# Other layouts of q, k and v on the partitions, at the start of a fused attention and MoE kernel

## The chip, the cores and the metric

The kernel runs on one core of a Trainium2 chip. The metric is the device time of one execution in microseconds. Before the change three runs took 1101.92, 1102.78 and 1104.07 us (median 1102.78 us).

## The reference

Three stages follow each other: linear attention with an RMS norm, a "max of three" MLP (below MoE 1), and a dense mixture of four experts (MoE 2). All data are float32.

```python
# q, k, v: (4, 8, 576, 64); g_norm: (64,)
kv  = einsum('bhsd,bhse->bhde', k, v)
out = einsum('bhsd,bhde->bhse', q, kv)
x   = out / sqrt(mean(out*out, -1) + 1e-6) * g_norm      # -> (2304 tokens, 512)
h   = maximum(maximum(x @ w1, x @ w2), x @ w3)           # MoE 1, d_ff = 768
x   = h @ w_out
p   = probs / (probs.sum(-1) + 1e-9)                     # 4 experts, d_ff = 1024
out = sum_e p[:, e] * (maximum(x @ e_w1[e], 0) @ e_w2[e])
```

## The kernel before

Products of the two MoE stages are taken with operands split in a high and a low part (`fp32r`), some by a seven-product scheme. They fill the time from about 60 us to the end and the change doesn't touch them. It touches the attention, which fills the first 60 us, and the order of the tokens inside a tile of 128.

**Groups and tiles.** Each of the four batches has 576 tokens. The first 512 make two groups of 256 tokens, each two tiles of 128; the last 64 tokens of two batches share one tile. `groups` numbers them 0 to 9: 0, 1 (batch 0), 2 (the rests), 3, 4 (batch 1), 5, 6 (batch 2), 7 (the rests again), 8, 9 (batch 3). The rests of all four batches are loaded and transposed together, as group 2. A group of 256 tokens is laid out with two neighbouring tokens on each of 128 partitions.

**Loads.** `load_q` (line 132) fetches a group with one DMA of 512 KB, whose contiguous pieces are two tokens of a head, 512 bytes; the rests come with four DMAs of 128 KB (line 138), each to 32 partitions. `load_kv` (line 169) fetches four heads of one batch of k and of v, here called a chunk: four neighbouring tokens on each of 128 partitions (pieces of 1 KB, line 175) and, by a second DMA of 64 KB, the last 64 tokens on 64 partitions (pieces of 256 bytes, line 176). So a chunk is four DMAs and 1.18 MB. The first chunk is cut finer (`load_first`). All these come from SyncE's queue (SP), except two from ScalarE's queue in the first chunk.

**Order of loads.** The list `order` (line 926) gives it: `w` is a weight of MoE 1, `k01` chunk 1 of batch 0, `q1` group 1. After each step of the work `pump` issues on from it, as far as buffers are free: six for q groups, three chunks.

**Order of work.** The list `steps` (line 972) is the program order of every engine. Its letters: `Kbc` is one pair of heads of k^T v for batch b (`att_kv`, line 272; five accumulating matmuls for each head), `Tn` the transposes of q group n (`att_T`, line 295), `On` the product with kv and the sums of squares (`att_O`), `Nn` the norm (`att_N`), `Xn` the transposes of the result (`att_X`), `S` the split of x, `c`, `d`, `s` the conversion of a weight, `A`, `H`, `P` parts of MoE 1. The beginning is `K00 K01 c0 d0 K02 K03 T1 O1 T0 N1 K10 K11 O0 X1 N0 T2 T3 K12 K13 X0 O3 S0 N3 O2 K20 T4 O4 s0 N2 T5 N4 K21`. In `T2` the rests are first copied by POOL into head-contiguous order (line 303), then transposed from the copy.

**Norm.** `att_O` sums squares into `ss` and computes `a = ss/64 + 1e-6` on VectorE; `att_N` takes the square root on ScalarE from `ss` with a scale and a bias, so beside `a`, and VectorE goes on with both.

Of the kernel before, what the change touches and what calls it, by code (L numbers as in the profile page):

```python
# [8 lines left out]
F32 = mybir.dt.float32  # L9
# [3 lines left out]
AF = mybir.ActivationFunctionType  # L13
# [8 lines left out]
def tile_attn_moe_moe2(  # L22
# [23 lines left out]
    nc = tc.nc  # L46
    B, H, S, D = q.shape
    NT, DM = out.shape
    FF = w1.shape[1]
    E, _, EF = e_w1.shape  # L50
    P = 128
# [5 lines left out]
    TPB = T // P  # L57
    NTILE = NT // P
    NPAIR = H // 2
    KC = S // P  # L60
    EPS = 1e-6
    WARM = 16

    def f32(ap):
# [25 lines left out]
    eps = cst.tile([P, 1], F32, name="eps")  # L90
    p_all = cst.tile([P, NTILE, E], F32, name="p_all")
# [24 lines left out]

    tiles = []
    groups = []
    SB = S // 256 * 256
    for b0 in range(0, B, 2):  # L120
        for b, s0 in ((b0, 0), (b0, 256), (b0, None), (b0 + 1, 0), (b0 + 1, 256)):
            groups.append((b, s0, len(tiles)))
            if s0 is None:
                tiles.append([out[bb * S + SB : (bb + 1) * S, :] for bb in (b, b + 1)])
            else:
                rows = out[b * S + s0 : b * S + s0 + 256, :].rearrange("(p r) d -> r p d", r=2)
                tiles += [[rows[0]], [rows[1]]]

    q_sb = {}
    kv_sb = {}  # L130

    def load_q(pool, gi):
        b, s0, _ = groups[gi]
        t = pool.tile([P, H, 2, D], F32, tag="q", name=f"q{gi}", bufs=6)
        if s0 is None:
            n = P // B
            for bb in range(B):
                nc.sync.dma_start(
                    out=t[bb * n : (bb + 1) * n], in_=q[bb, :, SB:S, :].rearrange("h (p r) d -> p h r d", r=2)
                )  # L140
        else:
            nc.sync.dma_start(
                out=t, in_=q[b, :, s0 : s0 + 256, :].rearrange("h (p r) d -> p h r d", r=2)
            )
        q_sb[gi] = t

    HALF = P // 2
    KS = P * KC  # L150

    def load_first(pool):

        ends = []
        for src, nm, eng in ((k, "k", nc.sync), (v, "v", nc.scalar)):
            t = pool.tile([P, 4, KC + 1, D], F32, tag="kv", name=f"{nm}0_0", bufs=6)
            rows = src[0, 0:4]
            parts = [
                (t[:, 2 * i : 2 * i + 2, 0:KC, :], rows[2 * i : 2 * i + 2, 0:KS, :].rearrange("h (p c) d -> p h c d", c=KC))
                for i in range(2)  # L160
            ]
            eng.dma_start(out=parts[0][0], in_=parts[0][1])
            eng.dma_start(out=t[0:HALF, :, KC, :], in_=rows[:, KS:S, :].rearrange("h p d -> p h d"))
            ends.append(parts[1])
            kv_sb[nm, 0, 0] = t
        for o, i in ends:
            nc.sync.dma_start(out=o, in_=i)

    def load_kv(pool, b, c):
        if (b, c) == (0, 0):  # L170
            return load_first(pool)
        for src, nm in ((k, "k"), (v, "v")):
            t = pool.tile([P, 4, KC + 1, D], F32, tag="kv", name=f"{nm}{b}_{c}", bufs=6)
            rows = src[b, 4 * c : 4 * c + 4]
            nc.sync.dma_start(out=t[:, :, 0:KC, :], in_=rows[:, 0:KS, :].rearrange("h (p c) d -> p h c d", c=KC))
            nc.sync.dma_start(out=t[0:HALF, :, KC, :], in_=rows[:, KS:S, :].rearrange("h p d -> p h d"))
            kv_sb[nm, b, c] = t

# [91 lines left out]
    def att_kv(kvb, b, c, eng=""):  # L272
        if c == 0:
            kv_ps[b] = banks[7]
        ps = kv_ps[b]
        kt, vt = kv_sb["k", b, c // 2], kv_sb["v", b, c // 2]
        for i in range(KC + 1):
            for h in range(2):
                o = ps[h * D : (h + 1) * D, c * D : (c + 1) * D]
                n = P if i < KC else HALF  # L280
                hh = c % 2 * 2 + h
                nc.tensor.matmul(o, kt[0:n, hh, i, :], vt[0:n, hh, i, :], start=(i == 0), stop=(i == KC))
        if c == NPAIR - 1:
            dst = kvb[b % 2][:, 0 : H * P].rearrange("p (c h n) -> p c h n", h=2, n=P)
            for h in range(2):
                src = ps[h * D : (h + 1) * D, 0 : NPAIR * D].rearrange("p (c e) -> p c e", e=D)
                e = eng[2 * h :] or "aa"
                copy(e[0], dst[0:D, :, h, 0:D], src)
                copy(e[1], dst[D:P, :, h, D:P], src)

    qT = {}
    TAIL = 2
    xtok = {}

    def att_T(pool, gi, eng="aa"):


        pair = groups[gi][1] is None
        t = pool.tile([P, 4, P, 2] if pair else [P, 2, 4, P], F32, tag="qp" if pair else "qT", name=f"qT{gi}", bufs=1 if pair else 2)
        qs = q_sb.pop(gi)  # L300
        if pair:
            qr = pool.tile([P, 2, H, D], F32, tag="qr", name="qr", bufs=1)
            nc.gpsimd.tensor_copy(out=qr, in_=qs.rearrange("p h r d -> p r h d"))
        for i in range(2):
            ps = bank("a").rearrange("p (c n) -> p c n", n=P)
            for c in range(4):
                src = qr[:, i, 2 * c : 2 * c + 2, :] if pair else qs[:, 4 * i + c, :, :]
                nc.tensor.transpose(ps[:, c, :], src, ident)
            copy(eng[i], t[:, :, :, i] if pair else t[:, i], ps)
        qT[gi] = t  # L310

    def att_O(pool, kvb, gi):
        b, s0, _ = groups[gi]
        qt = qT[TAIL] if s0 is None else qT.pop(gi)
        ps = [bank("acc") for i in range(1 if s0 is None else 2)]
        xt = pool.tile([P, 2, H, D], F32, tag="xt", name=f"xt{gi}", bufs=3)
        if s0 is None:
            nbank = 1
            for c in range(NPAIR):
                for bb in range(2):  # L320
                    rows = slice(bb * HALF, (bb + 1) * HALF)
                    toks = slice((b + bb) * P // B, (b + bb + 1) * P // B)
                    pair = kvb[(b + bb) % 2][:, 2 * c * P : 2 * c * P + 384]
                    nc.tensor.matmul(
                        ps[0][rows, c * P : (c + 1) * P], qt[:, c, toks, :],
                        pair.rearrange("p (h n) -> p h n", h=2)[:, :, 0:D], start=True, stop=True,
                    )
            dst = [xt[:, 0]]
        else:
            nbank = 2  # L330
            for h in range(H):
                nc.tensor.matmul(
                    ps[h // 4][:, h % 4 * P : (h % 4 + 1) * P], qt[:, h // 4, h % 4, :],
                    kvb[b % 2][:, h * P : (h + 1) * P], start=True, stop=True,
                )
            dst = [xt[:, :, 4 * i : 4 * i + 4, :].rearrange("p r h d -> p h r d") for i in range(2)]
        o = [ps[i].rearrange("p (n d) -> p n d", d=D) for i in range(nbank)]

        def small(nm):
            return smp.tile([P, nbank, 8], F32, tag=nm, name=f"{nm}{gi}")  # L340

        ss, a = small("ss"), small("a")
        for i in range(nbank):
            sq = xt[:, i]
            nc.scalar.activation(out=sq, in_=o[i], func=AF.Square)
            nc.vector.reduce_sum(out=ss[:, i, :], in_=sq, axis=AX.X)
        nc.vector.tensor_scalar(out=a, in0=ss, scalar1=1.0 / D, scalar2=EPS, op0=ALU.mult, op1=ALU.add)
        xtok[gi] = (xt, ss, a, o, dst, small)

    def att_N(gi):  # L350
# [1 line left out]
        nbank = len(o)  # L352
        s0, rr = small("s0"), small("rr")

        nc.scalar.activation(out=s0, in_=ss, func=AF.Sqrt, scale=1.0 / D, bias=eps)
        nc.vector.reciprocal(out=rr, in_=s0)
        nc.vector.tensor_tensor(out=rr, in0=a, in1=rr, op=ALU.mult)
        nc.vector.tensor_tensor(out=rr, in0=rr, in1=s0, op=ALU.add)
# [529 lines left out]
    def load_probs():  # L888
        for gi, (b, s0, t) in enumerate(groups):
            if s0 is None:  # L890
                for r in range(2):
                    nc.sync.dma_start(
                        out=p_all[r * HALF : (r + 1) * HALF, t, :], in_=probs[(b + r) * S + SB : (b + r + 1) * S, :]
                    )
            else:
                r0 = b * S + s0
                nc.sync.dma_start(
                    out=p_all[:, t : t + 2, :], in_=probs[r0 : r0 + 256, :].rearrange("(p r) e -> p r e", r=2)
                )

    def norm_probs():
# [6 lines left out]
    with tc.manual_schedule():  # L908
# [13 lines left out]
        for t in kvb:  # L922
# [1 line left out]


        order = (
            "w k00 k01 q1 q0 k10 q3 q2 k11 q4 q5 k20 w q6 k21 w k30 k31 q8 w q9"
        ).split()
        free = {"q": 6, "k": 3}

        def pump():
            late = []
# [51 lines left out]
        for st in steps:  # L984
# [10 lines left out]
                    conv2(worder[n], *en)  # L995
            elif kind == "T":
                att_T(xq, *at, *en)
                free["q"] += 1
            elif kind == "K":
                att_kv(kvb, *at, *en)  # L1000
                free["k"] += at[1] % 2
# [274 lines left out]
```

## Time and profile before

| what | value |
| --- | --- |
| median of 3 runs | 1102.78 us |
| the profiled execution, its own time | 1102.58 us |
| its span (first to last instruction) | 1100.8 us |
| TensorE (PE) busy | 1070.6 us, 97% |
| VectorE (DVE) busy | 768.7 us, 70% |
| ScalarE (ACT) busy | 593.9 us, 54% |
| GpSimd (POOL) busy | 238.8 us, 22% |
| granted TensorE clock, mean | 0.993 of full speed |

Busy shares are means over the whole span. The attention at the start has limits of its own, so tables by stretches of time are read for it. A matmul of float32 shows as two records in the trace. "L282" is line 282 of the kernel before.

### The profile page before, as it was taken

To read this page: it belongs to the slowest core of one execution; us is meant where nothing else is said; L and a number is where in the kernel's file an instruction comes from. 1 tells how busy PE (TensorE), PEld (TensorE's weight loads), DVE (VectorE), ACT (ScalarE), POOL (GpSimd) and SP (SyncE) were. 2 spreads that over 40 slices of the span, in tenths; PEclk is the share of its full clock that TensorE was granted. 3 is DMA by queue.
4 is the path that set the end of the run, shared out by engine and by line. 5 is a ranking of instruction groups with operands and counts; after the bars stand their busy time and mean duration, and the time that the engine had idled before them with its cause. 6 is when DMAs were issued, how large, how long until landed. Compare 5 with 4: busy or idle time off the path is not lost.

```text
span 1100.8 us, 19219 instructions
## 1 busy us (share of the span) xinstructions
PE 1070.6 (97%) x7318; PEld 1051.7 (96%) x7318; DVE 768.7 (70%) x1434; ACT 593.9 (54%) x1257; POOL 238.8 (22%) x269
## 2 busy tenths in 40 slices
PE   7889999999999989999999999999999999999997
PEld 6779999999999879999999999999999999999997
DVE  3889985667656879776676666667667666666556
ACT  3544224335343666665665566666566566556652
POOL 1336633330101101111202212212212220221121
PEclk8999999999999999999999999999999999999999
DMA  9945555431610877388569579759949957956875
GB/s 259 295 148 162 181 182 178 132 119 53 210 58 20 328 270 266 142 311 240 90 221 272 119 169 285 182 100 290 250 77 277 277 86 227 271 116 166 235 222 115
DMA packets 109820, 209.17 MB, mean 190 GB/s; under 512 B 13856, under 2 KB 67104, under 8 KB 109728
## 3 DMA queue, kind: packets, MB, share of 16 engines
q1 hardware_dynamic: 89248, 169.34, 46.4%
q0 software_dynamic: 19472, 37.76, 19.2%
q8 instruction: 57, 0.93, 0.3%
q10 hardware_dynamic: 1008, 0.85, 0.3%
q14 instruction: 35, 0.29, 0.1%
HBM read 137.93 MB, written 69.99 MB: 189 GB/s over the span
## 4 chain that ended last, share of the span: by engine, by line
PE 63%; DVE 0%; issue 0%; DVEq 0%
PE bank L878 32%; PE bank L617 30%; DVE wr L579 0%; DVE xr L500 0%; DVE fa L861 0%; DVE hr L653 0%; DVE hr L651 0%; DVEq L1271 0%
## 5 line engine op out<-in xcount | busy, mean ns | idle before, releaser
L878 PE MATMUL bank<-wr 128*128 128x256 f32 x1701 | 263.5, 283 | 0.4 <-DVE wr L579 0.4
L878 PEld LDWEIGHTS bank<-wr 128*128 128x128 f32 x1701 | 239.9, 190 | 0.6 <-DVE wr L579 0.6
L617 PE MATMUL bank<-rb,wl 128*128 128x384 f32 x1032 | 211.6, 340 | 4.2 <-DVE rb L500 2.3
L671 ACT ACTIVATE fa<-bank 128x384 f32<-128x384 f32 x192 | 94.7, 493 | 171.4 <-PE bank L617 169.5
L617 PEld LDWEIGHTS bank<-rb,wl 128*128 128x128 f32 x1032 | 176.0, 189 | 7.4 <-DVE rb L500 3.5
L617 PE MATMUL bank<-xr,wl 128*128 128x384 f32 x864 | 175.8, 337 | 1.7 <-DVE xr L500 1.1
L617 PEld LDWEIGHTS bank<-xr,wl 128*128 128x128 f32 x864 | 144.9, 188 | 3.6 <-DVE xr L500 2.5
L653 DVE TENSOR_TENSOR wr<-fa,wr 128x384 fp32r<-128x384 f32 x131 | 72.3, 552 | 50.8 <-ACT wr L646 50.7
L878 PE MATMUL bank<-wr,hr 128*128 128x256 f32 x558 | 91.0, 281 | 0.0
L836 POOL DMA_DIRECT2D out_dram<-w2s x48 | 48.1, 1027 | 193.0 <-DVE ob L861 145.0
L836 POOL DMA_DIRECT2D out_dram<-ob x48 | 47.7, 1033 | 166.8 <-DVE w2s L861 90.6
L878 PEld LDWEIGHTS bank<-wr,hr 128*128 128x128 f32 x558 | 80.5, 188 | 0.0
L646 ACT ACTIVATE wr<-fa 128x384 fp32r<-128x384 f32 x152 | 78.2, 529 | 2.0 <-DVE fa L661 0.5
L878 PE MATMUL bank<-wr,xr 128*128 128x256 f32 x405 | 67.9, 281 | 0.0
L760 DVE TENSOR_TENSOR fa<-bank,fa 128x384 f32<-128x384 f32 x54 | 29.9, 554 | 51.8 <-ACT fa L757 36.5
L836 POOL DMA_DIRECT2D out_dram<-fa x37 | 34.2, 1054 | 123.9 <-DVE fa L861 68.9
L694 DVE TENSOR_TENSOR fa<-bank,fa 128x384 f32<-128x384 f32 x48 | 26.7, 557 | 49.2 <-PE bank L617 49.2
L683 DVE TENSOR_TENSOR fa<-bank,fa 128x384 f32<-128x384 f32 x48 | 26.7, 557 | 48.0 <-ACT fa L671 47.2
L859 ACT ACTIVATE ob<-bank,p_all 128x256 f32<-128x256 f32 x102 | 48.3, 474 | 21.7 <-PE bank L878 20.0
L859 ACT ACTIVATE w2s<-bank,p_all 128x256 f32<-128x256 f32 x104 | 49.3, 474 | 18.8 <-PE bank L878 18.7
L617 PE MATMUL bank<-op,wl 128*128 128x384 f32 x288 | 58.7, 339 | 0.6 <-ACT fa L671 0.6
L878 PEld LDWEIGHTS bank<-wr,xr 128*128 128x128 f32 x405 | 59.0, 188 | 0.0
(207 smaller groups left out, 2041.9 us busy)
## 6 DMA issues: line engine op xcount, KB each, us to landing
rb<-op_d SPq DMA_DIRECT2D x42, 768.0 KB, 5.1
xr<-op_d SPq DMA_DIRECT2D x42, 768.0 KB, 7.0
out_dram<-w2s POOLq DMA_DIRECT2D x47, 256.0 KB, 5.9
out_dram<-ob POOLq DMA_DIRECT2D x46, 256.0 KB, 5.2
op<-op_d SPq DMA_DIRECT2D x14, 768.0 KB, 7.9
stage_a<-in_moe_w_dram SPq DMA_DIRECT2D x18, 512.0 KB, 4.0
w1s<-in_moe_w_dram SPq DMA_DIRECT2D x30, 256.0 KB, 3.6
out_dram<-fa POOLq DMA_DIRECT2D x30, 256.0 KB, 5.9
```

The lines of the kernel that those rows point to most:

```text
L617: nc.tensor.matmul(out, w[wi][:, c * P : (c + 1) * P], y[yi][:, c, :], start=(i == 0 and k in begin), stop=(i == 5), skip_group_check=k no ...
L646: nc.scalar.activation(out=ops[key][0], in_=src, func=AF.Relu if relu else AF.Copy)
L653: nc.vector.tensor_tensor(out=lo, in0=src, in1=f32(hi), op=ALU.subtract)
L671: nc.scalar.activation(out=out, in_=in_, func=func)
L683: nc.vector.tensor_tensor(out=t22, in0=x, in1=t22, op=ALU.add)
L694: nc.vector.tensor_tensor(out=t12, in0=x, in1=t12, op=ALU.add)
L760: nc.vector.tensor_tensor(out=mx[done] if i == 0 else t, in0=x, in1=t, op=ALU.add)
L836: nc.gpsimd.dma_start(out=rows, in_=src, accum_op=ALU.add)
L859: nc.scalar.activation(out=o, in_=piece(ps, i), func=AF.Copy, scale=pe)
L878: nc.tensor.matmul(piece(ps, i), h[hi][:, i * P : (i + 1) * P], w[wi], start=fresh, stop=last, skip_group_check=True,)
```

## The change

q of a batch is loaded as four tokens on each of 128 partitions, 512 tokens in two DMAs of four heads each (pieces of 1 KB); tiles and output rows follow that order. The rests come by eight DMAs of 64 KB, one for each batch and token of a pair (pieces of 256 bytes), already in the order that the transposes want, and POOL's copy is gone. k and v come with six tokens on each of 96 partitions, one DMA for each chunk and operand (pieces of 1.5 KB), without the second DMA; the matmuls contract over 96 rows, six for each head in place of five. The list of loads and the count of free q buffers follow; a q buffer comes free when both its groups are transposed. `a` now lies in the place of `ss`, and the square root reads it.

```diff
-    KC = S // P
+    KC = 6
+    KP = S // KC
-    SB = S // 256 * 256
+    SB = S // 512 * 512
+    by_r = [out[b * S : b * S + SB, :].rearrange("(p r) d -> r p d", r=4) for b in range(B)]
...
-                rows = out[b * S + s0 : b * S + s0 + 256, :].rearrange("(p r) d -> r p d", r=2)
-                tiles += [[rows[0]], [rows[1]]]
+                r0 = s0 // P
+                tiles += [[by_r[b][r0]], [by_r[b][r0 + 1]]]
...
+    def load_q(pool, b):
+        if b == B:
+            t = pool.tile([P, 2, H, D], F32, tag="qe", name="q_ends", bufs=1)
             n = P // B
             for bb in range(B):
+                for r in range(2):
+                    nc.sync.dma_start(
+                        out=t[bb * n : (bb + 1) * n, r],
+                        in_=q[bb, :, SB:S, :].rearrange("h (p r) d -> r p h d", r=2)[r],
+                    )
+            q_sb[TAIL] = t
+            return
+        t = pool.tile([P, H, 4, D], F32, tag="q", name=f"q{b}", bufs=3)
+        for i in range(2):
+            hs = slice(i * H // 2, (i + 1) * H // 2)
+            nc.sync.dma_start(out=t[:, hs], in_=q[b, hs, 0:SB, :].rearrange("h (p r) d -> p h r d", r=4))
+        for n, gi in enumerate(gi for gi, g in enumerate(groups) if g[0] == b and g[1] is not None):
+            q_sb[gi] = t[:, :, 2 * n : 2 * n + 2, :]
+
+    def load_kv(pool, b, c):
+        first = (b, c) == (0, 0)
         ends = []
+        for src, nm in ((k, "k"), (v, "v")):
+            t = pool.tile([P, 4, KC, D], F32, tag="kv", name=f"{nm}{b}_{c}", bufs=6)
+            rows = src[b, 4 * c : 4 * c + 4].rearrange("h (p c) d -> p h c d", c=KC)
+            if first:
+                (nc.sync if nm == "k" else nc.scalar).dma_start(out=t[0:KP, 0:2], in_=rows[:, 0:2])
+                ends.append((t[0:KP, 2:4], rows[:, 2:4]))
+            else:
+                nc.sync.dma_start(out=t[0:KP], in_=rows)
+            kv_sb[nm, b, c] = t
         for o, i in ends:
             nc.sync.dma_start(out=o, in_=i)
...
-        for i in range(KC + 1):
+        for i in range(KC):
             for h in range(2):
...
-                n = P if i < KC else HALF
                 hh = c % 2 * 2 + h
-                nc.tensor.matmul(o, kt[0:n, hh, i, :], vt[0:n, hh, i, :], start=(i == 0), stop=(i == KC))
+                nc.tensor.matmul(o, kt[0:KP, hh, i, :], vt[0:KP, hh, i, :], start=(i == 0), stop=(i == KC - 1))
...
-        if pair:
-            qr = pool.tile([P, 2, H, D], F32, tag="qr", name="qr", bufs=1)
-            nc.gpsimd.tensor_copy(out=qr, in_=qs.rearrange("p h r d -> p r h d"))
...
-                src = qr[:, i, 2 * c : 2 * c + 2, :] if pair else qs[:, 4 * i + c, :, :]
+                src = qs[:, i, 2 * c : 2 * c + 2, :] if pair else qs[:, 4 * i + c, :, :]
...
-        ss, a = small("ss"), small("a")
+        ss = small("ss")
+        a = ss
...
-        nc.scalar.activation(out=s0, in_=ss, func=AF.Sqrt, scale=1.0 / D, bias=eps)
+        nc.scalar.activation(out=s0, in_=a, func=AF.Sqrt)
...
-            "w k00 k01 q1 q0 k10 q3 q2 k11 q4 q5 k20 w q6 k21 w k30 k31 q8 w q9"
+            "w k00 k01 q0 k10 q4 k11 q1 k20 w q2 k21 w k30 k31 w q3"
-        free = {"q": 6, "k": 3}
+        free = {"q": 4, "k": 3}
+        got = set()
...
-                free["q"] += 1
+                mate = {0: 1, 1: 0, 3: 4, 4: 3, 5: 6, 6: 5, 8: 9, 9: 8}.get(at[0])
+                got.add(at[0])
+                free["q"] += mate in got
```

In the new list `q0` to `q3` are the batches and `q4` the rests. The loads of `probs` follow the new token order with pieces of the same size.

## Rows read from the trace of the kernel before

**Rows 1.** The page's busy times: engine, us (share of the span) x instructions.

```profile
PE 1070.6 (97%) x7318; PEld 1051.7 (96%) x7318; DVE 768.7 (70%) x1434; ACT 593.9 (54%) x1257; POOL 238.8 (22%) x269
```

**Rows 2.** Windows: stretch, its length, busy us by engine, clock, DMA share, GB/s.

```profile
core 0: us, PE busy (x) PEld busy (x) DVE busy (x) ACT busy (x) POOL busy (x), PEclk, DMA share, GB/s
...
10.00:15.00 5.00, 2.42 (x36) 2.15 (x36) 1.77 (x3) 0.00 (x0) 1.73 (x2) 0.76 1.11 283
...
40.00:50.00 10.00, 9.00 (x111) 7.75 (x110) 9.24 (x27) 7.02 (x16) 3.11 (x2) 1.00 1.12 304
50.00:60.00 10.00, 8.80 (x124) 8.02 (x123) 9.57 (x19) 4.86 (x11) 4.21 (x4) 1.00 1.16 300
...
70.00:140.00 70.00, 66.80 (x399) 64.54 (x398) 67.29 (x107) 24.79 (x46) 43.00 (x35) 1.00 0.48 149
```

**Rows 3.** Waits of PE, 0 to 62 us: total us, times, longest.

```profile
PE bank L282 <- DMA v<-in_v_dram: 5.9, 5, 2.9
PE bank L308 <- POOL qr L303: 1.8, 1, 1.8
```

**Rows 4.** Timeline of PE, 9 to 45 us: start, us, instructions, idle before.

```profile
12.58 2.98 PE L282 MATMUL bank<-v,k 128*64 128x64 f32 x40 [2.94 <-DMA v<-in_v_dram]
...
25.03 1.29 PE L375 MATMUL bank<-ident,xt 128*128 128x128 f32 x8
28.14 1.09 PE L308 MATMUL bank<-ident,qr 128*128 128x128 f32 x8 [1.82 <-POOL qr L303]
...
30.58 1.82 PE L282 MATMUL bank<-v,k 128*64 128x64 f32 x40 [0.39 <-DMA v<-in_v_dram]
...
38.14 0.95 PE L282 MATMUL bank<-v,k 128*64 128x64 f32 x20 [1.07 <-DMA v<-in_v_dram]
```

**Rows 5.** Timeline of VectorE, 30 to 45 us, same columns.

```profile
32.45 0.85 DVE L71 COPY kvb<-bank 64x256 f32<-64x256 f32 x2 [1.85 <-PE bank L282]
...
37.43 0.92 DVE L347 TENSOR_SCALAR a<-ss 128x16 f32<-128x16 f32 x1
```

**Rows 6.** Timeline of SyncE's queue, 0 to 33 us: start, us, DMAs issued.

```profile
0.72 0.45 SPq L203 DMA_DIRECT2D stage_a<-in_moe_w_dram  x1
...
8.58 0.61 SPq L176 DMA_DIRECT2D v<-in_v_dram  x1
...
14.44 0.61 SPq L176 DMA_DIRECT2D v<-in_v_dram  x1
15.10 0.60 SPq L142 DMA_DIRECT2D q<-in_q_dram  x1
15.75 5.53 SPq L138 DMA_DIRECT2D q<-in_q_dram  x4
...
24.43 0.61 SPq L176 DMA_DIRECT2D v<-in_v_dram  x1
```

**Rows 7.** Those DMAs' issues, in order of time: count, size, us from issue to landing.

```profile
stage_a<-in_moe_w_dram SPq DMA_DIRECT2D x1, 512.0 KB, 3.7
...
v<-in_v_dram SPq DMA_DIRECT2D x1, 64.0 KB, 4.3
...
v<-in_v_dram SPq DMA_DIRECT2D x1, 64.0 KB, 7.4
...
q<-in_q_dram SPq DMA_DIRECT2D x1, 512.0 KB, 9.3
...
v<-in_v_dram SPq DMA_DIRECT2D x1, 64.0 KB, 6.5
```

**Rows 8.** DMA traffic in 2.7-4.3, 22-23, 30.5-31.5 and 32.5-33.4 us.

```profile
DMA packets 603, 0.60 MB, mean 376 GB/s; under 512 B 16, under 2 KB 603, under 8 KB 603
...
DMA packets 403, 0.20 MB, mean 196 GB/s; under 512 B 20, under 2 KB 403, under 8 KB 403
...
DMA packets 569, 0.29 MB, mean 290 GB/s; under 512 B 2, under 2 KB 569, under 8 KB 569
...
DMA packets 348, 0.32 MB, mean 360 GB/s; under 512 B 14, under 2 KB 348, under 8 KB 348
```

More of the change, by code (lines that the diff above doesn't have):

```diff
@@ L59, in tile_attn_moe_moe2 @@
     NPAIR = H // 2
-    KC = S // P
+    KC = 6
+    KP = S // KC
     EPS = 1e-6
+    HALF = P // 2
     WARM = 16
@@ L118, in tile_attn_moe_moe2 @@
     groups = []
-    SB = S // 256 * 256
+    SB = S // 512 * 512
+    TAIL = 2
+    by_r = [out[b * S : b * S + SB, :].rearrange("(p r) d -> r p d", r=4) for b in range(B)]
     for b0 in range(0, B, 2):
@@ L125, in tile_attn_moe_moe2 @@
             else:
-                rows = out[b * S + s0 : b * S + s0 + 256, :].rearrange("(p r) d -> r p d", r=2)
-                tiles += [[rows[0]], [rows[1]]]
+                r0 = s0 // P
+                tiles += [[by_r[b][r0]], [by_r[b][r0 + 1]]]
     q_sb = {}
     kv_sb = {}
[L132 to L135, printed above, removed]
+    def load_q(pool, b):
+        if b == B:
+            t = pool.tile([P, 2, H, D], F32, tag="qe", name="q_ends", bufs=1)
@@ L136, in load_q @@
             n = P // B
             for bb in range(B):
[L138 to L152, printed above, removed]
-        ends = []
[L155 to L165, printed above, removed]
+                for r in range(2):
[3 more added lines that the diff above has]
+                    )
@@ L166, in load_first @@
         for o, i in ends:
             nc.sync.dma_start(out=o, in_=i)
[L169 to L177, printed above, removed]
@@ L291, in tile_attn_moe_moe2 @@
     qT = {}
-    TAIL = 2
     xtok = {}
@@ L895, in load_probs @@
             else:
-                r0 = b * S + s0
+                r0 = s0 // P
                 nc.sync.dma_start(
-                    out=p_all[:, t : t + 2, :], in_=probs[r0 : r0 + 256, :].rearrange("(p r) e -> p r e", r=2)
+                    out=p_all[:, t : t + 2, :],
+                    in_=probs[b * S : b * S + SB, :].rearrange("(p r) e -> p r e", r=4)[:, r0 : r0 + 2, :],
                 )
```

## The prediction, made before the changed kernel ran

> **What bounds the kernel now.** The page's busy times come first: PE is busy for 97% of the span [rows 1], so only time in which PE stands or is held back can be won. The stretches [rows 2] say where that is and what holds it. From 70 to 140 us PE and VectorE are both above 95%; from 40 to 60 us VectorE is at 94% and PE at 89%, while DMA runs at 1.1 of its engines' time and moves 300 GB/s. So there are three regimes at the start: until about 40 us data decides, from 40 to 140 us VectorE's program order, after that PE alone. The waits of PE [rows 3] name the data: 5.9 us for k and v in five waits, 1.8 us for POOL's copy. A DMA that lands sooner helps where PE and VectorE then run sooner; what VectorE gains by 40 us it carries on, since it has hardly any idle time left to lose it in. So the place to look is the last wait on data ahead of that: K12 and K13 (PE, 30.58 to 32.40 us, after a wait for v) [rows 4], which VectorE awaited for 1.85 us [rows 5]. The sum is made for the end of K13, 32.40 us.
>
> **When data lands now.** Issue [rows 6] plus time to landing [rows 7]: the first weight 0.72 + 3.7 = 4.4 us, the end of chunk 2 (v's 64 KB) 8.58 + 4.3 = 12.9, of chunk 3 14.44 + 7.4 = 21.8, of chunk 4 24.43 + 6.5 = 30.9. Between them lie two chunks; two q groups and a chunk; a q group, the rests and a chunk. A q group of 0.524 MB in pieces of 512 bytes takes 1.81 us at 290 GB/s, the rests 2.67 us at the 196 GB/s that the chip gave them on 32 partitions at 22 us [rows 8]. So the chunks cost 8.5, 21.8 - 12.9 - 3.6 = 5.3 and 30.9 - 21.8 - 1.8 - 2.7 = 4.6 us: 18.4 us for four, 4.6 us each, 256 GB/s. Pieces of 1 KB on 128 partitions ran at 360 GB/s [rows 8], by which a chunk without its 64 KB parts (1.05 MB) takes 2.9 us; the rest of the 4.6 us is the two small DMAs and what they disturb.
>
> **The change, part by part.**
> A chunk becomes two DMAs of 0.59 MB, pieces of 1.5 KB on 96 partitions. No row shows that shape. From below it is bounded by 196 GB/s (32 partitions), from above by 376 (a weight, 128 partitions) [rows 8]: 6.0 to 3.1 us. Nearest is the 360 GB/s of k and v on 128; I take a tenth off for the partitions left out, 320 GB/s, 3.7 us.
>
> A rule of the Trainium skill speaks against this part. The row: 512-byte pieces ran at 290 GB/s on 128 partitions, and at 196 on 32 [rows 8]. SBUF — State Buffer, section "Door 1: The DMA port swizzle", says that DMA reaches SBUF by 16 ports, that partitions 0 to 63 lie on eight of them and 64 to 127 on the others. Then 96 partitions load the first eight twice as much, and the ceiling is 12/16 of its 435 GB/s, an estimate of 326; for 32 partitions it gives 218, and the row's 196 agrees in direction and lies a tenth below. By 326 a chunk takes 3.6 us and the sum below hardly moves; scaled from the row (196 x 12/8 = 294) it takes 4.0 us, and K13 ends 1.2 us later than in the sum.
>
> q on 128 partitions in pieces of 1 KB: 360 instead of 290 GB/s, 1.46 instead of 1.81 us for 0.524 MB. The other way it could stay at 1.81.
>
> The rests: eight DMAs of 64 KB in 256-byte pieces. From the rests' own 196 GB/s 2.7 us; by the small DMAs of k and v, half of the chunk's 4.6 - 2.9 us each, 6.8 us for eight. I take 3.2, near the first, since the data and the 32 partitions are the same. They also hold the queue: v's part issued at 24.43 us went when the q group issued at 15.10 had landed (15.10 + 9.3 = 24.4), four rests and three issues lying between [rows 6, 7], so eight transfers are in flight at most. Eight rests are all of that with only 0.5 MB; at 5.53 us for four issues now, of which much is waiting, SP issues k and v of chunk 4 late. That may leave DMA idle for 0 to 1.3 us; the 0.5 us above 2.7 stands for it.
>
> Order: `q1` (two groups, 1.05 MB) now stands behind chunk 4, where group 3 stood before chunk 3 was used up; T3 is in front of K12 in PE's program, so T3 waits for both, and K12, K13, X0 and O3 stand behind T3.
>
> New landings: 4.4 + 2 x 3.7 = 11.8; q of batch 0 14.7; chunk 3 18.4; rests 21.6; chunk 4 25.3; first half of q1 26.8, second half 28.2.
>
> PE: each head takes 12 records for 10, so a pair of K steps 48 instead of 40: 0.36 us more at 1.82 us for 40 [rows 4], 2.9 us in all. Up to X1 that is 0.36 for K10 and K11 and 0.6 for K02 and K03, which run at half clock (2.98 us for 40). Against it K02 starts 0.9 us sooner, with the data (11.8 + as much as now). X1's end stays at 26.3. T2 follows at once, without POOL's copy: 1.8 us less, to 27.4. Half of T3 to 28.0, the other from 28.2 to 28.8, K12 and K13 2.2 us: 31.0, that is **1.4 us sooner**. What is late next is T3's second half of q1 by 0.2 us, so either more speed of PE or a little less of DMA is lost there.
>
> Behind it: the 1.07 us that K20 waits for v [rows 4] goes too (chunk 5 lands at 31.9), but VectorE paces PE there, so I count nothing. The remaining 1.6 us of added records lie beside VectorE's work between 38 and 57 us; without that cover they cost 1.6. The square root now starts behind one VectorE instruction (0.17 us, 0.92 with POOL beside it [rows 5]); VectorE has other work before it uses the root in most groups, so nothing to 0.9 us in all; I take 0.2 us for both. POOL's second of copying was in its idle time. The output's and the probabilities' new token order keeps pieces and counts: nothing, and nothing either way in the stages behind.
>
> Sum: 1102.58 - 1.4 + 0.2 = 1101.4 us against the profiled execution, which lies 0.2 us under the median: **1101.5 us**. A measurement of this kernel tells about 0.2%, 2.2 us, from no change. So this is no change that can be told.
>
> **Rivals.**
> 1. *The loads are faster than I take them: faster.* At 376 GB/s a chunk takes 3.1 us, v of chunk 2 lands at 10.7, and PE's idle time ahead of K02, 2.94 us now, shrinks to about 1 us. After that idle the clock was low (0.76 over 10 to 15 us [rows 2]) and 40 records took 2.98 instead of 1.82 us [rows 4]; if it stays up, T2 ends at about 24, q1 lands at 26.0, and K13 ends at 28.8: 3.6 us sooner, 1099.2. For it: fewer DMAs, larger pieces, and rows at 360 and 376. Against it: 196 GB/s where partitions were few.
> 2. *T3 waits and the clock falls there: slower.* At 280 GB/s or less (4.2 us for a chunk) q1's halves land at 28.8 and 30.3, PE stands for 2.4 us about T3 and K13 ends at 33.1, 0.7 late. An idle time of 2.9 us was followed by half clock; then K12, K13, X0 and O3, some 6 us of PE, take some 3.4 us longer, of which K20's 1.07 us gives back one: 3.0 us later, 1105.6. It decides from about 290 GB/s on. For it: q1 behind chunk 4, the narrow transfers' 196. Against it: behind the 1.8 us of idle ahead of T2 the 40 records of K12 and K13 took 1.82 us, the full rate [rows 4].
> 3. *It doesn't do what it says:* the DMA stage gets shorter but VectorE's order takes it up, the root's wait and the added K records cost what is won by 32 us: 1102.6. For it: VectorE's 94% from 40 us on and 96% to 140 us.
>
> **How the numbers follow.** My sum 0.40 (alone 1100.3 to 1103.3), the fast loads 0.30, T3's wait 0.17, nothing won 0.13. Faster by over 2.2 us: nearly all of the second and a fifth of the first, 0.37. Slower by that: the third and the edge of the first and the last, 0.20. Within: 0.43. The range goes from 1098.6, a little past the fast case, to 1105.6, the slow one; the far bound of 6 us for a chunk is left out, as chunk and piece are nothing like that row.
>
> **What would show it.** In the profile after: v of chunk 2 landing near 11.8 us; chunk and q rates of 320 and 360 GB/s; no POOL wait ahead of T2; T3's second half waiting for q by some tenths; K13's end near 31.0; the same difference at the start of VectorE's chain behind O3 and at 140 us. Wrong if the clock's low stretch goes, or moves behind T3; if chunks take over 4.2 or under 3.3 us; or if the difference at 32 us isn't that at 140.

## The result, and the profile after

The changed kernel took 1115.6 us (median of 4 runs, 1111.29 to 1117.2), beside 1103.12 us for the kernel before (4 runs, 1101.92 to 1104.07): ratio 1.0105, 95% interval 1.0082 to 1.0128. It is **slower by 1%**, 12.5 us, and lies outside the range of 1098.6 to 1105.6 us. The profiled execution took 1115.22 us with a span of 1113.4, so the two profiles differ by 12.6 us and can stand for the medians.

The busy time of the engines hardly explains it. The page, as [rows 1]:

```profile
PE 1073.4 (96%) x7382; PEld 1056.3 (95%) x7382; DVE 769.3 (69%) x1434; ACT 593.0 (53%) x1257; POOL 238.7 (21%) x268
```

PE is busy for 2.8 us more; the other 9.8 us are time in which it stands. The windows show where (columns as in [rows 2]):

```profile
10.00:15.00 5.00, 0.92 (x24) 0.81 (x24) 1.81 (x3) 0.00 (x0) 1.11 (x1) 0.63 1.11 221
...
30.00:35.00 5.00, 0.41 (x4) 0.17 (x2) 2.19 (x7) 1.39 (x4) 0.00 (x0) 1.00 1.10 294
35.00:40.00 5.00, 3.04 (x26) 2.37 (x28) 0.69 (x1) 0.60 (x1) 0.00 (x0) 0.52 1.12 236
40.00:50.00 10.00, 9.75 (x113) 9.20 (x110) 5.10 (x9) 4.44 (x9) 3.30 (x3) 0.73 1.10 282
50.00:60.00 10.00, 8.43 (x122) 7.56 (x121) 9.28 (x25) 7.10 (x16) 2.94 (x2) 1.00 1.11 263
...
70.00:140.00 70.00, 65.55 (x392) 63.06 (x391) 62.48 (x101) 27.99 (x51) 39.58 (x32) 0.96 0.46 139
```

From 30 to 35 us PE works 0.41 us of 5. The granted clock, the column after POOL's, is at 1.00 there and at 0.52, nearly the lower level of 1.2 GHz, in the five us after that idle time. From 10 to 15 us the DMA share is 1.11, as it was before, but only 221 GB/s move instead of 283: the DMA engines are as busy and move less. Between 40 and 50 us VectorE works 5.10 us, where it worked 9.24 before [rows 2], since its work comes about 10 us later.

The waits of PE over 0 to 62 us, as [rows 3] (total us, times, longest):

```profile
PE bank L272 <- DMA v<-in_v_dram: 8.0, 4, 4.0
PE bank L294 <- DMA q<-in_q_dram: 6.6, 2, 5.3
```

POOL's 1.8 us are gone, as foreseen; the wait for q, 0.3 us before, is 6.6 us now. In the timeline of PE, as [rows 4] (start, us, instructions, idle before):

```profile
15.43 2.83 PE L272 MATMUL bank<-v,k 96*64 96x64 f32 x48 [3.98 <-DMA v<-in_v_dram]
...
24.87 1.62 PE L272 MATMUL bank<-v,k 96*64 96x64 f32 x48 [1.14 <-DMA v<-in_v_dram]
...
28.31 1.04 PE L362 MATMUL bank<-ident,xt 128*128 128x128 f32 x8
29.18 1.22 PE L294 MATMUL bank<-ident,q_ends 128*128 128x128 f32 x8
35.74 1.08 PE L294 MATMUL bank<-ident,q 128*128 128x128 f32 x4 [5.34 <-DMA q<-in_q_dram]
38.05 1.09 PE L294 MATMUL bank<-ident,q 128*128 128x128 f32 x4 [1.22 <-DMA q<-in_q_dram]
39.06 2.83 PE L272 MATMUL bank<-v,k 96*64 96x64 f32 x48
```

In order: K02 and K03 start 2.8 us later than before, T2 follows X1 without a gap, then the two halves of T3 wait 5.34 and 1.22 us for the two halves of `q1`, and K12 and K13 run behind them at half clock (the granted clock from 39.1 to 41.9 us is 0.50) and end at 41.9 us. Before, they ended at 32.40: **9.5 us late at the place for which the sum was made**. VectorE's next step shows the same, against 32.45 us in [rows 5]:

```profile
41.94 0.85 DVE L73 COPY kvb<-bank 64x256 f32<-64x256 f32 x2 [4.38 <-PE bank L272]
```

Set side by side, equal instructions of VectorE are mostly 9.5 to 9.7 us later than before, from 43 to 115 us (9.1 to 10.4 us for single ones). The remaining 3 us are lost between 120 and 143 us in this one execution. ScalarE's waits there for the store of a converted weight (`w_da`), before (108 to 134 us) and after (118 to 146 us):

```profile
ACT cv_a L224 <- DMA w_da<-cv_a: 0.4, 1, 0.4
...
ACT cv_a L215 <- DMA w_da<-cv_a: 5.9, 2, 3.8
```

The first of the two, 3.8 us, stands where ScalarE had waited 3.1 us for VectorE, and VectorE is 10.4 us late behind it; the second, 2.2 us, stands where it had waited 0.4, and behind it VectorE is 12.3 us late. In the profiles of the five kernels below in which PE contracts over 96 rows, 1.6 to 3.4 us are lost in this place, and in those with k and v as before 0.6 us at most. Why the stores are late there, no run shows.

Now the transfers. SyncE's queue, as [rows 6] (start, us, DMAs issued), and what those DMAs took from issue to landing, as [rows 7]:

```profile
4.66 0.31 SPq L165 DMA_DIRECT2D v<-in_v_dram  x1
...
10.78 0.80 SPq L165 DMA_DIRECT2D v<-in_v_dram  x1
...
13.28 11.79 SPq L142 DMA_DIRECT2D q_ends<-in_q_dram  x8
...
25.61 0.48 SPq L165 DMA_DIRECT2D v<-in_v_dram  x1
26.13 1.03 SPq L151 DMA_DIRECT2D q<-in_q_dram  x2
```

```profile
v<-in_v_dram SPq DMA_DIRECT2D x1, 576.0 KB, 10.7
...
v<-in_v_dram SPq DMA_DIRECT2D x1, 576.0 KB, 14.0
...
v<-in_v_dram SPq DMA_DIRECT2D x1, 576.0 KB, 7.0
```

So v of chunk 2 lands at 4.66 + 10.7 = 15.4 us (forecast 11.8), of chunk 3 at 24.8 (18.4), of chunk 4 at 32.6 (25.3), and the halves of `q1`, by the starts of T3, at 35.7 and 38.0 (26.8 and 28.2). SP spends 11.8 us on the issue of the rests, much of it waiting: the seventh goes out at 21.85 us and the eighth at 24.75, as k and v of chunk 3 land (21.8 and 24.8), each the eighth DMA ahead of it in the queue. DMA traffic, as [rows 8], in 10-13, 18-21.5, 23-25, 32.5-34 and 45-49 us:

```profile
DMA packets 432, 0.64 MB, mean 212 GB/s; under 512 B 17, under 2 KB 432, under 8 KB 432
...
DMA packets 496, 0.75 MB, mean 215 GB/s; under 512 B 16, under 2 KB 495, under 8 KB 495
...
DMA packets 1168, 0.30 MB, mean 149 GB/s; under 512 B 1155, under 2 KB 1168, under 8 KB 1168
...
DMA packets 513, 0.53 MB, mean 350 GB/s; under 512 B 15, under 2 KB 512, under 8 KB 512
...
DMA packets 633, 0.92 MB, mean 230 GB/s; under 512 B 20, under 2 KB 633, under 8 KB 633
```

The first two and the last are k and v, nearly all in pieces of 1.5 KB on 96 partitions: 212, 215 and 230 GB/s. The third is the rests. The fourth is q on 128 partitions: 350 GB/s.

### The profile page after: what moved, and what is told of

Same layout as the page of the kernel before. It is cut to its first block, busy times and chain, and to the rows that moved or that the text cites. A ratio compares the mean times of both kernels' runs of the same rounds, so it can differ in the third digit from the quotient of the medians.

```text
span 1113.4 us, 19330 instructions
## 1 busy us (share of the span) xinstructions
PE 1073.4 (96%) x7382; PEld 1056.3 (95%) x7382; DVE 769.3 (69%) x1434; ACT 593.0 (53%) x1257; POOL 238.7 (21%) x268
## 4 chain that ended last, share of the span: by engine, by line
PE 62%; DVE 0%; issue 0%; DVEq 0%
PE bank L865 32%; PE bank L604 30%; DVE wr L566 0%; DVE xr L487 0%; DVE fa L848 0%; DVE hr L640 0%; DVE hr L638 0%; DVEq L1262 0%
## 5 line engine op out<-in xcount | busy, mean ns | idle before, releaser
L681 DVE TENSOR_TENSOR fa<-bank,fa 128x384 f32<-128x384 f32 x48 | 26.8, 557 | 49.0 <-PE bank L604 49.0
L670 DVE TENSOR_TENSOR fa<-bank,fa 128x384 f32<-128x384 f32 x48 | 26.8, 557 | 48.0 <-ACT fa L658 47.1
L517 POOL TENSOR_TENSOR w1s<-w1s 128x256 f32<-128x256 f32 x40 | 35.6, 909 | 109.9 <-DMA w1s<-in_moe_w_dram 49.0
```

The lines of the kernel that those rows point to most:

```text
L517: eng.tensor_tensor(out=st[o], in0=st[a], in1=st[b], op=ALU.subtract)
L670: nc.vector.tensor_tensor(out=t22, in0=x, in1=t22, op=ALU.add)
L681: nc.vector.tensor_tensor(out=t12, in0=x, in1=t12, op=ALU.add)
```

## The experiments

**Theory A**: the loss is the layout of k and v, whose transfers are slow (by the number of partitions, A1, or by the size of the piece, A2). **Theory B**: it is the rests, whose eight small DMAs fill the queue so that chunk 4 and `q1` are issued late. **Theory C**: it is the new order, with `q1` behind chunk 4. Medians are given with the ratio to the kernel before, run beside on the same chip (1104.81 us in the first four, 1104.12 in the next four, 1103.46 in the last four). The rows are those of one profiled execution, whose own time is given where it lies far from the median. With four runs of a kernel 0.2 to 0.5% can be told, with ten about 0.1%; kernels with one run have no interval, and only their rows are used. The new place of `a` is part of several of these kernels and was not tried alone.

**k and v as before, all else changed.**

```diff
-    KC = 6
-    KP = S // KC
+    KC = S // P
 ...
+            nc.sync.dma_start(out=t[:, :, 0:KC, :], in_=rows[:, 0:KS, :]...)
+            nc.sync.dma_start(out=t[0:HALF, :, KC, :], in_=rows[:, KS:S, :]...)
```

> The changed kernel with k and v loaded as before (four tokens on 128 partitions and the last 64 tokens by a small DMA); q, the rests, the order of loads and the square root stay changed. Theory A (the transfers to 96 partitions are what costs: 5.4 us a chunk in the changed kernel's landings against 4.6): four chunks to K12 give back 3 to 5 us and the low clock around T3 gets shorter, 1106 to 1110 us. Theory B (the eight small DMAs of the rests hold the queue, the layout of k and v is worth little): less than 2.5 us back, 1112 us or more. Theory C (order: T3 waits for q1 behind chunk 4 and the clock falls): as B, 1112 or more, with the low clock after T3 unchanged.

1107.84 us (6 runs), 1.0031 [1.0018, 1.0045]. Of the 12.5 us 3.0 are left (1107.84 - 1104.81). DMA traffic in 20 to 25 us, then two steps of PE's timeline:

```profile
DMA packets 1687, 0.53 MB, mean 105 GB/s; under 512 B 1532, under 2 KB 1687, under 8 KB 1687
```

```profile
31.00 0.74 PE L308 MATMUL bank<-ident,q 128*128 128x128 f32 x4 [3.28 <-DMA q<-in_q_dram]
...
33.52 2.99 PE L286 MATMUL bank<-v,k 128*64 128x64 f32 x40
```

The wait ahead of T3 and the half clock behind it are still there, 5.5 us earlier. The rests alone now leave the DMA engines idle (share 0.59 in that stretch, in which 105 GB/s move).

**k and v alone, on the kernel before.** The edit of `a` in the place of `ss` is in it too.

```diff
-    KC = S // P
+    KC = 6
+    KP = S // KC
 ...
-                nc.tensor.matmul(o, kt[0:n, hh, i, :], vt[0:n, hh, i, :], ...)
+                nc.tensor.matmul(o, kt[0:KP, hh, i, :], vt[0:KP, hh, i, :], ...)
```

> The kernel before with only k and v on 96 partitions (and the square root read from a, which makes room); q, the rests, POOL's copy and the order of loads as before. Theory A: a chunk takes about 5.3 us instead of 4.6, K13 ends 3 to 5 us later than in the kernel before, 1105 to 1109 us. Theory B and theory C: K13 ends within 1.5 us of the kernel before, 1101 to 1104.5 us.

1115.85 us (4 runs; the profiled one 1118.83), 1.0111 [1.0087, 1.0134]: by itself the whole loss. PE's waits over 0 to 62 us, and its timeline:

```profile
PE bank L268 <- DMA v<-in_v_dram: 12.9, 6, 4.3
```

```profile
35.24 1.62 PE L268 MATMUL bank<-v,k 96*64 96x64 f32 x48 [0.37 <-DMA v<-in_v_dram]
...
45.80 1.55 PE L268 MATMUL bank<-v,k 96*64 96x64 f32 x24 [4.28 <-DMA v<-in_v_dram]
```

Without the new order nothing waits for q; v is awaited six times instead, 12.9 us for 5.9 in [rows 3]. K13 ends 4.5 us late, as theory A foresaw, but the loss goes on behind it and is far more than the forecast of 1105 to 1109 us: VectorE is 4.4 us late at 43 us and 12.4 us at 62. So the layout decides, and the order only says where the lateness shows.

**The rests in four DMAs, with POOL's copy, all else changed.**

```diff
-                for r in range(2):
-                    nc.sync.dma_start(out=t[bb * n : (bb + 1) * n, r], ...)
+                nc.sync.dma_start(out=t[bb * n : (bb + 1) * n], ...)
```

> The changed kernel with the rests in four DMAs of 128 KB and POOL's copy again (into a free xt buffer); all else changed. Theory B (the eight DMAs of the rests let the queue run dry): SP's issue of the rests falls from 11.8 to about 6 us, the stretch from 23 to 27 us at 120 to 145 GB/s goes, 5 to 8 us back, 1108 to 1111 us. Theory A: 1 to 3 us back, 1112.5 to 1115. Theory C: 2 us or less.

1115.01 us (4 runs, 1110.22 to 1121.81, which is the profiled one), 1.0104 [1.0059, 1.0148]. PE's timeline:

```profile
35.93 1.09 PE L295 MATMUL bank<-ident,q 128*128 128x128 f32 x4 [5.53 <-DMA q<-in_q_dram]
```

Nothing comes back that can be told, and T3 waits as before. As the main cause, B falls.

**`q1` ahead of chunk 4, all else changed.**

```diff
-            "w k00 k01 q0 k10 q4 k11 q1 k20 w q2 k21 w k30 k31 w q3"
+            "w k00 k01 q0 k10 q1 q4 k11 k20 w q2 k21 w k30 k31 w q3"
```

> The changed kernel with batch 1 of q loaded ahead of the rests and of chunk 4 (order k10 q1 q4 k11); nothing else differs. Theory C (T3 waits behind chunk 4): PE's 5.3 us of idle time ahead of T3 is shared out, T3's transposes lie beside chunk 4's transfer, and the low clock after it gets shorter, 4 us or more back, 1111 us or less. Theories A and B: the data that K12 needs is the same, so the wait moves to T2 and K12, 0 to 2.5 us back, 1113 to 1116 us.

1113.95 us (4 runs; the profiled one 1117.04), 1.0086 [1.0065, 1.0108], an interval that overlaps the changed kernel's and leaves out the 1111 us or less of theory C. PE's timeline:

```profile
37.33 2.83 PE L272 MATMUL bank<-v,k 96*64 96x64 f32 x48 [4.59 <-DMA v<-in_v_dram]
```

The wait has moved from T3 to K12 and cost nearly as much: what is short is bandwidth, and another order hands on the lack.

**Pieces of 1.5 KB on all 128 partitions.** The rows loaded are others than the layout asks for, a third more bytes, and PE uses 96 partitions of them, so the attention's values are not those of the inputs.

```diff
+            at = min(b * H * S + 4 * c * S, B * H * S - 4 * P * KC)
+            rows = src.rearrange("b h s d -> (b h s) d")[at : at + 4 * P * KC, :]
+            rows = rows.rearrange("(h p c) d -> p h c d", h=4, c=KC)
 ...
-                nc.sync.dma_start(out=t[0:KP], in_=rows)
+                nc.sync.dma_start(out=t, in_=rows)
```

> The changed kernel, where each k and v DMA fills 128 partitions with pieces of 1.5 KB from other rows of k and v (1.57 MB a chunk instead of 1.18, a third more; the attention's values are therefore not those of the inputs; PE still contracts over 96 rows). Theory A1 (96 partitions reach the SBUF ports unevenly): traffic during k and v rises from some 225 GB/s to 340 or more, packets of 1.5 KB take 65 to 80 ns instead of 120, and the kernel is faster than the changed one despite the added bytes: K13 ends near 40 us instead of 41.9. Theory A2 (pieces of 1.5 KB, or reading in steps of 1.5 KB, are slow themselves): 220 to 250 GB/s as now, K13 ends at 47 us or later, 1120 us or more.

1111.86 us (one run). DMA traffic in 9-11.5, 22-26 and 34-36 us, then PE's timeline:

```profile
DMA packets 674, 0.99 MB, mean 398 GB/s; under 512 B 27, under 2 KB 674, under 8 KB 674
...
DMA packets 1062, 0.32 MB, mean 79 GB/s; under 512 B 1013, under 2 KB 1062, under 8 KB 1062
...
DMA packets 509, 0.75 MB, mean 374 GB/s; under 512 B 16, under 2 KB 509, under 8 KB 509
```

```profile
34.03 0.69 PE L296 MATMUL bank<-ident,q 128*128 128x128 f32 x4 [4.67 <-DMA q<-in_q_dram]
```

The same pieces that ran at 212 to 230 GB/s on 96 partitions run at 374 to 398 on 128. In the first stretches 674 packets went in 2.5 us, against 432 in 3 us, at a like DMA share (1.07 and 1.11 in 10 to 15 us), so each packet takes nearly twice the time on 96. So A1 and not A2. Other rows of k and v are read here, but the kernel before read the changed kernel's rows on 128 partitions, at 360 GB/s [rows 8]. K13 ends at 39.4 us, 2.5 us earlier, but the one run lies among the changed kernel's own (1111.29 to 1117.2), so a gain in the whole time isn't shown: the rests starve the DMA engines here (79 GB/s), and T3 still waits 4.7 us.

**Pieces of 2.25 KB on 64 partitions.** Room for two chunks instead of three, nine K records a head.

```diff
-    KC = 6
+    KC = 9
 ...
-        free = {"q": 4, "k": 3}
+        free = {"q": 4, "k": 2}
```

> The changed kernel with k and v as nine tokens (pieces of 2.25 KB) on each of 64 partitions, with room for two chunks instead of three. Theory A1 (ports): half of the ports, so 218 GB/s by the page's rule against 326 for 96 partitions; scaled from the rests' row (196 on half of the ports) 196 against 294. If 64 partitions run at the 225 GB/s of 96, the share of the ports is not what sets the 96. Theory A2 (size of the pieces): larger pieces are faster, 300 GB/s or more, and chunk 4 lands ahead of the changed kernel's 32.6 us.

1127.55 us (one run). Traffic in 10-13 us:

```profile
DMA packets 284, 0.59 MB, mean 198 GB/s; under 512 B 26, under 2 KB 26, under 8 KB 284
```

Fewer partitions, a little slower still, despite larger pieces. How much of the 1127.55 is the third chunk's missing room stays open.

**q's part alone**: k and v as before, the rests in four with the copy.

```diff
 (as in the first experiment, and)
-                for r in range(2):
-                    nc.sync.dma_start(out=t[bb * n : (bb + 1) * n, r], ...)
+                nc.sync.dma_start(out=t[bb * n : (bb + 1) * n], ...)
```

> k and v as before, the rests in four DMAs with POOL's copy (into a free xt buffer), q of a batch in pieces of 1 KB and the changed order of loads and square root. Against the run with k and v as before and the rests in eight: theory B (eight small DMAs let the queue run dry, 105 GB/s from 20 to 25 us there) gives 1.5 to 3 us back, 1105 to 1106.5 us; theory C (q1 behind chunk 4) leaves it at 1107.5 or more.

1107.1 us (10 runs), 1.0023 [1.0014, 1.0033], between the forecasts of B and C. PE's timeline:

```profile
31.02 0.63 PE L309 MATMUL bank<-ident,q 128*128 128x128 f32 x4 [3.06 <-DMA q<-in_q_dram]
...
33.68 2.91 PE L284 MATMUL bank<-v,k 128*64 128x64 f32 x40
```

T3 waits 3.06 and 1.14 us for q here, and K12 and K13 run at half clock, though the rests are in four and k and v as before. So q as a batch behind chunk 4 is itself a small loss.

**q's part alone, with `q1` ahead of the rests and chunk 4**, and the last batch ahead of the last weight.

```diff
-            "w k00 k01 q0 k10 q4 k11 q1 k20 w q2 k21 w k30 k31 w q3"
+            "w k00 k01 q0 k10 q1 q4 k11 k20 w q2 k21 w k30 k31 q3 w"
```

> As the run before it (q alone, rests in four), with batch 1 of q ahead of the rests and of chunk 4 and the last batch of q ahead of the last weight. Theory C: T3 no longer waits, the low clock behind it goes, 2 us or more faster than the run before it: 1102 to 1105 us, level with the kernel before or up to 2 us faster. Theory B: no difference between the two.

1105.22 us (10 runs), 1.0014 [1.0003, 1.0024].

```profile
30.61 1.09 PE L309 MATMUL bank<-ident,qr 128*128 128x128 f32 x8 [2.76 <-POOL qr L304]
...
33.34 1.82 PE L284 MATMUL bank<-v,k 128*64 128x64 f32 x40 [0.69 <-DMA v<-in_v_dram]
```

K12 is at full clock again, but the rests are now late, and T2 waits 2.76 us for POOL's copy of them. It is the fastest version with q in batches, 0.14% slower than the kernel before.

**Pieces of 1.5 KB on 112 partitions**, with other rows again. Readings of A1: the port with the most partitions sets the pace (A1a), as the prediction read the Trainium skill's SBUF — State Buffer, "Door 1: The DMA port swizzle", or a transfer is slow as soon as its partitions don't divide into whole eights for the 16 DMA engines (A1b).

```diff
+            KQ = 112
+            at = min(b * H * S + 4 * c * S, B * H * S - 4 * KQ * KC)
 ...
-                nc.sync.dma_start(out=t[0:KP], in_=rows)
+                nc.sync.dma_start(out=t[0:KQ], in_=rows)
```

> As the run with 128 partitions and pieces of 1.5 KB, but on 112 partitions (1.38 MB a chunk; the attention's values are not those of the inputs). Theory A1a (the busiest port sets the pace, each port taking what its partitions ask: 112 partitions use 14/16 of the ports' rate, 96 use 12/16): 320 GB/s or more while k and v run. Theory A1b (a transfer is slow as soon as its partitions don't divide into whole eights, one for each of the 16 DMA engines, so that engines meet on a port): 200 to 260 GB/s, as with 64 and 96 partitions.

1117.93 us (one run). Traffic in 10-12 and 18-20.5 us:

```profile
DMA packets 345, 0.51 MB, mean 253 GB/s; under 512 B 16, under 2 KB 345, under 8 KB 345
...
DMA packets 433, 0.66 MB, mean 263 GB/s; under 512 B 15, under 2 KB 432, under 8 KB 432
```

Leaving out one eighth of the partitions costs about a third of the rate. That is far from the 320 GB/s or more of A1a and at the upper edge of A1b's 200 to 260.

**Rests ahead of group 3, on the kernel before.**

```diff
-            "w k00 k01 q1 q0 k10 q3 q2 k11 q4 ...
+            "w k00 k01 q1 q0 k10 q2 q3 k11 q4 ...
```

> The kernel before with the rests loaded ahead of group 3 (order k10 q2 q3 k11), nothing else. If POOL's copy ahead of T2 (1.8 us of PE's idle time) holds K12: up to 1.5 us faster, 1102.5 to 1103.5 us beside 1104 for the kernel before. If K12's data is what ends last there (as the 0.39 us that it still waits for v says): no difference, 1103.5 to 1104.5.

1104.0 us (11 runs), 1.0001 [0.9992, 1.0009]: no difference. K12 takes over the wait, 1.81 us for v.

**The last 64 tokens of k and v once for each batch**, with that order.

```diff
-            nc.sync.dma_start(out=t[0:HALF, :, KC, :], in_=rows[:, KS:S, :]...)
+            if c == 0:
+                te = pool.tile([HALF, H, D], F32, tag="ke", name=f"{nm}e{b}", bufs=4)
+                nc.sync.dma_start(out=te, in_=src[b, :, KS:S, :]...)
```

> As the run with the rests first, and the last 64 tokens of k and of v come once for a batch (128 KB, all eight heads) instead of once for each chunk (64 KB): eight small DMAs fewer, 128 partitions for everything else. If the narrow transfers are what costs in the kernel before too (theory A): their bytes are the same and the data of K02 and K12 lands up to 1 us sooner, 1102 to 1103.5 us; if it is the number of DMAs (theory B): 2 us or more faster than the kernel before.

1105.03 us (11 runs), 1.0006 [0.9995, 1.0017]: no difference. Half as many small DMAs, the aim of the change to k and v without its 96 partitions, win nothing that can be told; neither forecast came.

**The rests in eight DMAs and without the copy, alone.**

```diff
+                for r in range(2):
+                    nc.sync.dma_start(out=t[bb * n : (bb + 1) * n, r], ...)
-            qr = pool.tile([P, 2, H, D], F32, tag="qr", name="qr", bufs=1)
-            nc.gpsimd.tensor_copy(out=qr, in_=qs.rearrange("p h r d -> p r h d"))
```

> The kernel before with only the rests changed: eight DMAs of 64 KB token by token, POOL's copy gone. Theory B (eight small DMAs let the queue run dry): chunk 4 lands 2 to 4 us later and T2 no longer waits for POOL, 1 to 3 us slower, 1105 to 1107 us. Theory A alone: within 1 us of the kernel before.

1105.18 us (10 runs; the profiled one 1107.03), 1.0014 [1.0004, 1.0024]. SP's queue, traffic in 25-28 us, PE's timeline:

```profile
15.65 9.72 SPq L139 DMA_DIRECT2D q<-in_q_dram  x8
```

```profile
DMA packets 570, 0.32 MB, mean 106 GB/s; under 512 B 338, under 2 KB 570, under 8 KB 570
```

```profile
33.30 2.90 PE L284 MATMUL bank<-v,k 128*64 128x64 f32 x40 [4.28 <-DMA v<-in_v_dram]
```

The 1.8 us of POOL's wait are won, but k and v of chunk 4 are issued later, K12 waits 4.28 us instead of 0.39, and its 40 records go at half clock (0.52).

## Why the prediction was wrong

**The step that failed is the chunk at 320 GB/s, 3.7 us.** It ran at 212 to 230 GB/s, so 1.18 MB take 5.1 to 5.6 us. Four chunks by 25.3 us at 1.4 to 1.9 us more each are 5.6 to 7.6 us, and chunk 4 landed 7.3 us after its forecast. The lateness didn't grow evenly: 3.6 us at chunk 2, 6.4 at chunk 3 with q of batch 0 before it, 7.3 at chunk 4 with the rests before it. Putting k and v back left 3.0 of 12.5 us, k and v alone made the whole loss. The bounds were right: 196 to 376 GB/s. The choice in them was not. It leaned on the row with the same operands and a like piece, 360 GB/s on 128 partitions, and called the row with few partitions "nothing like" the chunk. The runs at 128 and 96 partitions with the same piece show that the number of partitions was what counted, so the far row was the near one.

The rule weighed there, from the Trainium skill's SBUF — State Buffer, "Door 1: The DMA port swizzle", spoke in the right direction and not far enough. The section counts the ports that a range of partitions reaches; that the port with the most partitions sets the pace is the prediction's reading of its map. By that reading the ceilings, estimates from the section's 435 GB/s, are 326 GB/s for 96 partitions, 381 for 112 and 218 for 64. The runs measured 212 to 230, 253 to 263 and 198. For 96 and 112 the measurement decides against that reading as the whole account; for 64 it agrees, the row a tenth below.

**Rival 2 named the mechanism, and its price was too small.** T3 waited from 30.4 us, the clock fell, and T3, K12 and K13 ran at half speed, as it says. It took the chunk at 280 GB/s; at 5.5 us a chunk its own reckoning puts `q1`'s second half at 28.2 + 7.2 = 35.4 us and not 30.3. It landed at 38.0, since its two halves took 5.4 us behind chunk 4 and not 2.9: q's pieces ran at 350 GB/s while alone, and 996 of the 1024 had started by 35 us, but the last 28 started one behind the other until 37.1, with the next chunk beside them. With the 2.83 us of K12 and K13 and the 1.09 of T3, all at half clock, that is the end at 41.9 us. Its chance of 0.17 came from the same choice of the chunk's rate.

**The rests at 3.2 us, with 0 to 1.3 us of empty queue**, was large enough in the changed kernel: chunk 4 landed 7.8 us behind chunk 3, and 5.1 to 5.6 of that is the chunk's own, which leaves 2.2 to 2.7 us for the rests. The four DMAs in their place gave nothing back. With k and v on 128 partitions the eight do more harm: the DMA share fell to 0.59 (20 to 25 us, k and v as before) and 0.41 (25 to 28 us, the rests alone). The rests alone cost 0.14%, some 1.5 us, after the 1.8 us of POOL's wait that they win. Eight issues took SP 8.5 to 14.8 us in the kernels that have them, against 5.53 us for four in [rows 6].

**Right:** q in pieces of 1 KB, 350 GB/s for the 360 forecast; no wait for POOL ahead of T2; the place, the end of K13; and that VectorE carries on what is lost there, mostly 9.5 to 9.7 us from 43 to 115 us, which also sends rival 3 (its order takes the difference up) away. The last 3 us, at the stores of weights, no step had.

**Wrong without weight:** the twelve records for ten. They were put at 0.36 us a pair at full clock; 48 records over 96 rows took 1.62 us where 40 took 1.82 [rows 4]. The 72 over 64 rows of the kernel with 64 partitions took 2.31 us, so a record over 64 rows takes about as long as one over 96, 32 to 34 ns; the 45 ns before belong to steps that mix matmuls over 128 and over 64 rows. Why those take longer, no run shows.

**Rival 1** needed the rate of 376 and the idle time ahead of K02 to shrink; it grew from 2.94 to 3.98 us. Even where that rate was there (374 to 398 GB/s on 128 partitions, clock 0.90 in 10 to 15 us), T3's wait remained; that kernel also moved a third more of k and v, so how much of the win the order takes at the right size stays open.

The parts don't add up: k and v alone cost 1.11%, q alone 0.23%, the rests alone 0.14%, all together 1.05%. K13 ends 4.5, 4.2 and 3.8 us late in the profiles of the three and 9.5 us in the changed kernel's; that what waits once does not wait again is argued, not shown.

## What to carry to other kernels

When a transfer's shape is not in the profile, look for the row that shares its partitions, not the one that shares its operand or piece, and if two rows are as far apart as 196 and 376 GB/s, keep both in the range. Where data decides, removing small DMAs is worth less than keeping all 128 partitions. Before an order is blamed, put it back alone: with too little bandwidth the wait only moves to the next instruction that needs data.

## What the runs showed of the hardware

The rate of loads by the number of partitions, in the stretches shown, with the engines busy throughout:

| partitions | piece | GB/s |
| --- | --- | --- |
| 32 (kernel before) | 512 bytes | 196 |
| 64 | 2.25 KB | 198 |
| 96 | 1.5 KB | 212 to 230 |
| 112 | 1.5 KB | 253 to 263 |
| 128 | 512 bytes | 290 |
| 128 | 1 KB | 350 to 376 |
| 128 | 1.5 KB | 374 to 398 |

From 112 to 128 the rate goes up by 40 to 60%. Only the rows of 1.5 KB, and those of 512 bytes, hold the piece the same. Why the rate falls, the runs don't show: a packet on fewer partitions takes longer, but no record says what it waits for.

Eight small DMAs in a row can empty the queue: with 0.5 MB in eight of them 79 to 106 GB/s moved in the stretches behind them. In the changed kernel the last two of the eight went out only as the DMA eight places ahead of each landed (21.85 and 24.75 us against 21.8 and 24.8), and k and v of chunk 4 stand behind them. Whether the chip or the program sets this eight, no run shows.
